# One quarter of w_in converted early, token groups changed every eight steps

## The chip, the core and the metric

One core of one Trainium2 chip runs the whole program in one launch. The metric is the device time of one execution in microseconds (us). The engines are TensorE (PE in the profile; PEld is its weight loads), VectorE (DVE), ScalarE (ACT), GpSimd (POOL) and SyncE (SP, which here only issues DMAs). Each engine runs its own instructions in the order in which they were written down, and they wait for each other by semaphores.

## The reference, cut to what matters

Three layers follow each other: windowed attention with 32 global tokens per batch, a soft mixture of experts, and a feed-forward layer whose weights w_in and w_out come as float64.

```python
# attention: 4 batches, 8 heads, 512 local + 32 global tokens, window 32
x = attention(q_l, k_l, v_l, q_g, k_g, v_g)      # (2176, 512)
logits = x @ phi                                 # 8 experts x 4 slots = 32 columns
slot_input = softmax(logits, 0).T @ x            # (8, 4, 512)
slot_out[e] = relu(slot_input[e] @ w1[e]) @ w2[e]
x = softmax(logits, 1) @ slot_out                # (2176, 512)
h = relu(x @ w_in)                               # w_in (512, 2048)
out = (h * h) @ w_out                            # w_out (2048, 512)
```

## The kernel before, in words

**Attention and the loads beside it.** The attention runs over 44 units of scores, exponent, transpose and product with V. The order of all work is the order of the code: tables tell after which unit a helper is emitted. In the shadow of the attention SP loads the expert weights in 64 pieces of 512 KB (`load_piece`, L581, in the order of the list `order`) into granules of 4 KB per partition. A granule is one place for one piece or one block; the lists in `room` hold the free ones: 16 of arena A, 8 and later more of arena B. Where no granule is free the load waits until a product has read one out.

**Conversion.** w_in and w_out arrive as float64 and are turned into single precision by five pieces of work (`convert`, L535): `split` (ACT, L540), `rest` (ACT L551 or DVE L553), `clamp` and `shift` (DVE, L543 and L546), and `join` (DVE L556, then an addition on POOL, L558). A w_out block is also cut into a high and a low half, `w_hl` (ACT L859, POOL L860). The left half of w_in, eight blocks of 128x512, is converted within the attention, at the units in `CONV` (L302), through one raw buffer: each block is loaded when the one before it is done.

**Experts.** `layer1` and `layer2` multiply the few slot rows with the 64 pieces; PE goes through 4 pieces at a time. After the last of them (`layer2(1, 6, 8)`) the result `so` is copied out, transposed (`layer2_T`) and becomes `slot_outT`. In `layer2` one idle product of 512 columns (L955) stands after the seventh of the eight parts.

**The last layer.** x is not built. G = slot_out @ w_in (32 rows) is split into a high and a low half and repeated (`G4`), so that one product gives a block of 128 features of h for 384 tokens. The work goes in 48 steps; a step is one token group (768, 768 or 640 tokens) with one of 16 blocks of features. `emit_h(n)` makes h of step n: a product (PE L1085), a relu (ACT L1088), a multiplication (DVE L1089); `emit_h_split(n)` cuts h*h into `ah` (ACT L1095) and `al` (DVE L1096). `emit_o(n)` then adds three products for each of six (or five) token tiles (PE L1140 to L1142) into six PSUM buffers. Round n of the loop holds `emit_h(n)`, then `emit_o(n-1)`, then what `plan[n]` holds of the conversions. `passes` (L1067) sets which group runs over which blocks; where a group stops before its last block its six sums are copied to `saved` and added later (L1147).

**What is converted there.** `seq` lists 24 raw blocks: eight of w_out, eight of w_in, eight of w_out. Block q begins in round q-2 (`split`, `rest`), goes on in round q-1 and, for w_out, ends in round q. `G_late` (L1027) makes the second half of G in two calls, at steps 11 and 15, and `replicate` (L1032) one eighth of G4 at a time. Both take a PSUM buffer of the pool `ps_h`, which has two and which the products of `emit_h` use as well.

Of the kernel before, what the change touches and what calls it, by code (L numbers as in the profile page):

```python
# [24 lines left out]
def local_global_attention__soft_moe__relu2_kernel(  # L25
# [51 lines left out]
    GR = 1024  # L77
# [31 lines left out]
    win_sb = A.carve(NC, FF // 2)  # L109
# [23 lines left out]
    room = {"a": A.granules(7, 23), "b": Bq.granules(10, 18), "t": []}  # L133
# [138 lines left out]
    for s in range(NJ):  # L272
# [29 lines left out]
    CONV = (4, 9, 13, 18, 22, 27, 31, 36)  # L302
    CONV_AT = (
        (0, 0, 1, 2, 3), (-1, 1, 1, 2, 3), (0, 0, 1, 2, 3), (0, 0, 0, 2, 3), (0, 1, 1, 2, 3), (0, 0, 0, 2, 3),
        (0, 1, 2, 2, 3), (0, 0, 1, 1, 2),
    )
    REST_ON_ACT = (0, 0, 1, 0, 1, 1, 1, 1)
# [5 lines left out]
        0, 0, 0, 0, 1, 2, 0, 0, 1, 1, 1, 1, 0, 1, 1, 1, 0, 0, 2, 2, 1, 0, 1, 1, 0, 1, 2, 1, 0, 1, 0, 0,  # L313
        3, 1, 0, 1, 1, 0, 1, 0, 4, 2, 2, 1,
# [262 lines left out]
    order.insert(62, ("raw", 0, 0))  # L577
# [3 lines left out]
    def load_piece():  # L581
# [8 lines left out]
        at = next((r for r in ("tba" if kind == 2 and e >= 4 else "tab") if room[r]), None)  # L590
# [25 lines left out]
    with tc.manual_schedule():  # L616
# [53 lines left out]
        for n in range(NC * WRES):  # L670
# [4 lines left out]
            if n + 1 < NC * WRES:  # L675
                after(u, win_load, n + 1, d=CONV_AT[n][-1])
# [5 lines left out]
        after(("l", 11, 1), give, "at", 6, 7, d=av_at(index["l", 11, 1]) - index["l", 11, 1] + MOE_D[2])  # L682
# [72 lines left out]
        free("at", 5, 6)  # L755
# [56 lines left out]
        tmp, = A.granules(4, 5)  # L812
# [12 lines left out]
        seq = [("o", m) for m in range(8)] + [("i", k) for k in range(2 * NC)] + [("o", m) for m in range(8, NFC)]  # L825
        plan = {}

        def raw_load():
            q = len(raws)
            if q == len(seq) or not room["a"]:  # L830
                return False
            raws[q] = g = room["a"].pop(0)
# [3 lines left out]
            else:  # L836
                f, c = WRES + k // NC, k % NC
# [7 lines left out]
        def put_convert(q, rest_on_act, first=False):  # L845
# [4 lines left out]
            else:  # L850
                f, c = divmod(k, NC)
# [10 lines left out]
            def last():  # L862
                join()
                room["a"].append(raws[q])
                raw_load()
# [346 lines left out]
```

## Time and profile before

| | us |
|---|---|
| median of 3 runs | 432.63 |
| lowest, highest | 430.64, 437.59 |
| the profiled execution's own time | 432.63 |
| its span | 430.2 |
| PE busy (share of the span) | 400.4 (93%) |
| DVE busy | 288.6 (67%) |
| ACT busy | 239.6 (56%) |
| POOL busy | 133.0 (31%) |

The span is the part of the profiled execution from its first to its last instruction. Busy PE contains products that overlap in the pipeline, so 93% is not a distance from a limit. The stages follow each other: attention to about 157 us, the passage to the experts to 169, the experts to 206, and from 210 on the last layer. The shares of busy time differ between them, so each is read by itself. A line number (L540) is one of the kernel before; the changed kernel's own numbers are a little different.

### The profile page before, as it was taken

What the parts mean: (1) busy time and instruction counts of PE and PEld (TensorE: products, weight loads), DVE (VectorE), ACT (ScalarE), POOL (GpSimd) and SP (SyncE); (2) the same over time, 40 slices, a digit from 0 to 9 for tenths busy, and PEclk for the clock granted to TensorE, in tenths of its full rate; (3) what the DMA queues carried; (4) which work ended last, traced back from release to release, by engine and by line L of the source; (5) the groups of instructions that cost most, each with busy time, mean ns of one, the idle gap of its engine ahead of it and who ended that gap; (6) DMA issues with size and microseconds to landing.
All of it is one profiled execution on the core that took longest, in us unless ns stands there. A gap on an engine that the chain in (4) does not pass through costs nothing.

```text
span 430.2 us, 12437 instructions
## 1 busy us (share of the span) xinstructions
PE 400.4 (93%) x4899; PEld 306.4 (71%) x4899; DVE 288.6 (67%) x930; ACT 239.6 (56%) x561; POOL 133.0 (31%) x159
## 2 busy tenths in 40 slices
PE   7789879989969978998999999999999999999996
PEld 6678667766757753354577877878877888888884
DVE  5597877768657866112599999778996545744443
ACT  3678768887867441221567666565754544444442
POOL 6245543644525531110345533234552000000000
PEclk9999999999989998999999999999999999999999
DMA  6888877899463698999913323300001500420003
GB/s 148 205 255 226 278 230 216 311 249 334 126 207 117 200 368 317 386 407 407 367 56 108 132 94 118 115 20 0 2 0 31 118 0 0 100 48 2 0 1 122
DMA packets 54890, 69.02 MB, mean 160 GB/s; under 512 B 23856, under 2 KB 40496, under 8 KB 54832
## 3 DMA queue, kind: packets, MB, share of 16 engines
q1 hardware_dynamic: 53360, 67.19, 48.2%
q10 hardware_dynamic: 1472, 1.05, 0.9%
q8 instruction: 38, 0.62, 0.6%
q14 instruction: 20, 0.16, 0.1%
HBM read 63.77 MB, written 4.46 MB: 159 GB/s over the span
## 4 chain that ended last, share of the span: by engine, by line
PE 62%; DVE 12%; DMA 11%; ACT 6%; issue 5%; SPq 1%; POOL 1%; POOLq 0%; ACTq 0%; DVEq 0%
PE ops L1140 9%; PE ops L1141 9%; PE ops L1142 9%; PE xp L391 5%; PE sp L330 5%; PE pp L372 4%; DMA arena_v<-in_v_l_dram 4%; DMA arena_a<-in_moe_w_out_dram 4%; PE hps L919 3%; PE tp L219 3%; PE ops L947 3%; DVE arena_a L543 3%; DMA arena_b<-in_moe_w_in_dram 3%; PE hp L1085 2%; ACT arena_b L146 2%
## 5 line engine op out<-in xcount | busy, mean ns | idle before, releaser
L1140 PE MATMUL ops<-w_hl,ah 128*128 128x512 f32 x271 | 107.2, 396 | 0.0
L1141 PE MATMUL ops<-w_hl,ah 128*128 128x512 f32 x271 | 106.3, 392 | 0.4 <-POOL w_hl L860 0.4
L1142 PE MATMUL ops<-w_hl,al 128*128 128x512 f32 x271 | 105.7, 390 | 0.0
L1089 DVE TENSOR_TENSOR arena_a<-hp,arena_a 128x384 f32<-128x384 f32 x96 | 46.8, 529 | 46.1 <-ACT arena_a L1088 46.0
L1088 ACT ACTIVATE arena_a<-hp 128x384 f32<-128x384 f32 x96 | 40.2, 471 | 66.0 <-PE hp L1085 65.9
L1095 ACT ACTIVATE ah<-arena_a 128x384 fp32r<-128x384 f32 x96 | 45.0, 505 | 25.9 <-DVE arena_a L1089 25.9
L1142 PEld LDWEIGHTS ops<-w_hl,al 128*128 128x128 f32 x271 | 50.9, 188 | 11.3 <-DVE al L1096 0.3
L1140 PEld LDWEIGHTS ops<-w_hl,ah 128*128 128x128 f32 x271 | 50.9, 188 | 11.0 <-issue 0.8
L1141 PEld LDWEIGHTS ops<-w_hl,ah 128*128 128x128 f32 x271 | 50.9, 188 | 10.5 <-POOL w_hl L860 1.8
L354 POOL TENSOR_TENSOR arena_r<-arena_b,nm 128x512 f32<-128x512 f32 x32 | 39.6, 1239 | 56.7 <-DVE nm L341 31.6
L1096 DVE TENSOR_TENSOR al<-arena_a,ah 128x384 fp32r<-128x384 f32 x96 | 49.9, 560 | 8.1 <-ACT ah L1095 4.2
L146 ACT ACTIVATE arena_b<-tp 64x256 f32<-64x256 f32 (+2 forms) x151 | 48.4, 347 | 9.3 <-PE tp L219 4.2
L558 POOL TENSOR_TENSOR arena_a<-arena_a 128x512 int32<-128x512 int32 x23 | 29.7, 1293 | 51.2 <-DVE arena_a L556 48.6
L341 DVE CUSTOM_DVE_ANT_0 arena_b<-sp,arena_r 128x128 f32<-128x128 f32 x128 | 29.5, 286 | 17.8 <-PE sp L330 11.9
L330 PE MATMUL sp<-arena_b 64*32 64x128 f32 x1024 | 36.0, 279 | 1.7 <-ACT arena_b L146 1.7
L391 PE MATMUL xp<-arena_v,arena_t 128*32 128x65 f32 x1408 | 27.6, 223 | 9.1 <-DMA arena_v<-in_v_l_dram 4.4
L364 ACT ACTIVATE arena_r<-arena_r 128x512 f32<-128x512 f32 x44 | 27.7, 630 | 10.5 <-POOL arena_r L354 10.2
L330 PEld LDWEIGHTS sp<-arena_b 64*32 64x32 f32 x1024 | 27.0, 110 | 9.1 <-issue 6.5
L372 PE MATMUL pp<-ident,arena_r 128*128 128x128 f32 x176 | 29.1, 289 | 4.4 <-ACT arena_r L364 4.4
L391 PEld LDWEIGHTS xp<-arena_v,arena_t 128*32 128x32 f32 x1408 | 22.4, 110 | 15.2 <-issue 11.0
L860 POOL TENSOR_TENSOR w_hl<-arena_a,w_hl 128x512 fp32r<-128x512 f32 x16 | 21.4, 1336 | 32.1 <-DMA arena_a<-in_moe_w_out_dram 16.2
L372 PEld LDWEIGHTS pp<-ident,arena_r 128*128 128x128 f32 x176 | 18.9, 142 | 10.9 <-ACT arena_r L364 5.4
(194 smaller groups left out, 589.5 us busy)
## 6 DMA issues: line engine op xcount, KB each, us to landing
arena_a<-in_moe_w_dram SPq DMA_DIRECT2D x35, 512.0 KB, 6.6
arena_b<-in_moe_w_dram SPq DMA_DIRECT2D x21, 512.0 KB, 7.2
arena_a<-in_moe_w_out_dram SPq DMA_DIRECT2D x16, 512.0 KB, 5.1
arena_v<-in_v_l_dram SPq DMA_DIRECT2D x16, 256.0 KB, 4.2
arena_b<-in_moe_w_in_dram SPq DMA_DIRECT2D x8, 512.0 KB, 4.9
arena_a<-in_moe_w_in_dram SPq DMA_DIRECT2D x8, 512.0 KB, 4.1
arena_k<-in_k_l_dram SPq DMA_DIRECT2D x30, 128.0 KB, 3.9
arena_q<-in_q_l_dram SPq DMA_DIRECT2D x30, 128.0 KB, 3.6
```

Source lines behind the costliest of these rows:

```text
L146: nc.scalar.activation(out=out, in_=in_, func=AF.Copy)
L330: nc.tensor.matmul(sp[r + 32 * e:r + 32 * e + 32, j], qz[d, (s + 2) % 3, hp, b], keys, start=True, stop=True, tile_position=(64 * e, r + 3 ...
L354: nc.gpsimd.tensor_tensor(out=pe.rearrange("p j (r k) -> p j k r", k=4), in0=s_buf.rearrange("p j (k r) -> p j k r", k=4), in1=nm.unsqueez ...
L372: nc.tensor.transpose(pp[:, j], pe_buf[n % NPE][:, j], ident)
L391: nc.tensor.matmul(xp[32 * b:32 * b + 32, 2 * h + e], p, V[:, b, 4 * half + 2 * h + e], start=True, stop=True)
L1088: nc.scalar.activation(out=r[:, :N], in_=hp[:, :N], func=AF.Relu)
L1089: nc.vector.tensor_tensor(out=a[:, :N], in0=hp[:, :N], in1=r[:, :N], op=ALU.mult)
L1095: nc.scalar.activation(out=ah[:, s], in_=a, func=AF.Copy)
L1096: nc.vector.tensor_tensor(out=al[:, s], in0=a, in1=ah[:, s].bitcast(F32), op=ALU.subtract)
L1140: nc.tensor.matmul(op, ah[:, s], w_hi, start=begin, stop=False)
L1141: nc.tensor.matmul(op, ah[:, s], w_lo, start=False, stop=False)
L1142: nc.tensor.matmul(op, al[:, s], w_hi, start=False, stop=end)
```

## The change

Only the first quarter of w_in (four blocks of 128x512) is converted within the attention. The other three quarters are converted in the last layer, which therefore has 28 blocks in `seq`: four of w_out, four of w_in, and so on in turn. Two granules of arena A that held w_in become room for pieces. The last layer changes token groups after 4, 8, 8, 8 and 4 steps, both of the first groups with partial sums. G is made in quarters, at steps 6, 14 and 22. The first block of w_out is loaded after all 64 pieces; `rest` of the last layer's blocks is always on ACT, and in round 3 two blocks begin at once.

```diff
-    win_sb = A.carve(NC, FF // 2)
+    CW = 512
+    win_sb = A.carve(NC, CW)
-    room = {"a": A.granules(7, 23), "b": Bq.granules(10, 18), "t": []}
+    room = {"e": [], "a": A.granules(10, 23), "b": Bq.granules(10, 18), "c": A.granules(5, 10), "t": []}
-    CONV = (4, 9, 13, 18, 22, 27, 31, 36)
+    CONV = (4, 9, 13, 18)
-    REST_ON_ACT = (0, 0, 1, 0, 1, 1, 1, 1)
+    REST_ON_ACT = (0, 0, 1, 0)
     PIECES = (
-        0, 0, 0, 0, 1, 2, 0, 0, 1, 1, 1, 1, 0, 1, 1, 1, 0, 0, 2, 2, 1, 0, 1, 1, 0, 1, 2, 1, 0, 1, 0, 0,
-        3, 1, 0, 1, 1, 0, 1, 0, 4, 2, 2, 1,
+        0, 0, 0, 0, 1, 2, 0, 0, 1, 1, 1, 1, 0, 1, 1, 1, 0, 0, 2, 2, 1, 1, 1, 1, 0, 2, 2, 1, 0, 1, 1, 0,
+        3, 1, 1, 0, 1, 0, 1, 1, 3, 1, 1, 1,
     )
-    order.insert(62, ("raw", 0, 0))
+    order.append(("raw", 0, 0))
...
-        seq = [("o", m) for m in range(8)] + [("i", k) for k in range(2 * NC)] + [("o", m) for m in range(8, NFC)]
+        seq = []
+        for f in range(NFC // 4):
+            if f:
+                seq += [("i", NC * f + c) for c in range(NC)]
+            seq += [("o", m) for m in range(4 * f, 4 * f + 4)]
...
-            a, b, c = q - 2, q - 1, q
+            b, c = a + 1, a + 2
...
-                if gr and c == 6:
-                    idle_products(1, ps_h, "h", c_flat[:, :512])
...
+        layer2(1, 2, 6)
...
+        put_convert(0, 0, True, True)
+        put_convert(1, 0, True)
+        now(("split", 0))
+        layer2(1, 6, 8)
+        while raw_load():
+            pass
+        now(("mask", 0), ("rest", 0))
...
         layer2_T(1)
+        now(("join", 0), ("split", 1), ("rest", 1))
...
+        sel = w_pool.tile([128, 2, 4, NS], F32R, name="sel")
+        nc.gpsimd.tensor_scalar(out=sel.rearrange("p a r s -> p (a r) s"), in0=blk.unsqueeze(1).to_broadcast([128, 8, NS]),
+                                scalar1=0.0, scalar2=None, op0=ALU.mult)
+        for r in range(4):
+            nc.gpsimd.tensor_copy(out=sel[:, r // 2, r], in_=blk)
+        now(("part", 0))
...
-        def G_late(j0, j1):
+        def G_late(f):
             gp = ps_h.tile([128, 256], F32, tag="h", name="gps")
-            G_part(1, gp, 0, NC, j0, j1)
-            G_split(1, gp, j0, j1)
+            G_part(f, gp, 0, NC)
+            G_split(f, gp)
...
-        passes = [(0, 0, 8), (1, 0, 16), (0, 8, 16), (2, 0, 16)]
+        passes = [(0, 0, 4), (1, 0, 8), (0, 4, 12), (1, 8, 16), (0, 12, 16), (2, 0, 16)]
-        late_at = {11: (0, 2), 15: (2, 4)}
+        late_at = {first_of[4 * f] - 2: f for f in range(1, 4)}
...
-                if t == 2 and n in late_at:
-                    G_late(*late_at[n])
-                if t == (4 if n == 0 else 3) and n in replicate_at:
+                if t == 1 and n in late_at:
+                    G_late(late_at[n])
+                if t == (4 if n == 0 or n in late_at else 3) and n in replicate_at:
                     replicate(replicate_at[n])
...
-                    if split and m == NFC - 1:
+                    if gi < 2 and (gi, 0, m + 1) not in passes:
                         nc.vector.tensor_tensor(out=o, in0=op, in1=o, op=ALU.add)
...
-            if n + 2 < len(seq):
-                put_convert(n + 2, n % 2 == 1 or n == 16)
+            for q in (n + 2,) if n < 3 else (5, 6) if n == 3 else (n + 3,):
+                if q < len(seq):
+                    put_convert(q, n, True)
...
-                for f in plan.pop(-5):
-                    f()
-                sel = w_pool.tile([128, 2, 4, NS], F32R, name="sel")
...
+                now(("mask", 1), ("join", 1))
+            if n == 1:
+                now(("part", 1))
```

SP's last loads before the stores, from the load into the freed V buffer on (arena_v), stand so before (moe_w holds w1 and w2):

```order
L599 DMA arena_v<-in_moe_w_dram 128x1024 x2
L599 DMA arena_b<-in_moe_w_dram 128x1024 x2
L599 DMA arena_t<-in_moe_w_dram 128x1024 x3
L599 DMA arena_a<-in_moe_w_dram 128x1024 x17
L599 DMA arena_b<-in_moe_w_dram 128x1024 x3
L533 DMA arena_a<-in_moe_w_out_dram 128x1024
L599 DMA arena_a<-in_moe_w_dram 128x1024
L599 DMA arena_t<-in_moe_w_dram 128x1024
L533 DMA arena_a<-in_moe_w_out_dram 128x1024 x7
```

and so in the changed kernel:

```order
L591 DMA arena_v<-in_moe_w_dram 128x1024 x2
L591 DMA arena_b<-in_moe_w_dram 128x1024 x2
L591 DMA arena_t<-in_moe_w_dram 128x1024 x3
L591 DMA arena_a<-in_moe_w_dram 128x1024 x17
L591 DMA arena_b<-in_moe_w_dram 128x1024 x2
L591 DMA arena_a<-in_moe_w_dram 128x1024
L531 DMA arena_a<-in_moe_w_out_dram 128x1024 x4
```

From V on, 30 loads end with the last piece before, and 27 now: two pieces fewer, and the w_out block behind them.

On ACT, rounds 2 to 4 of the last layer stood so before (L1088 is the relu, L1095 `ah`, L859 the high half of a w_out block, L540 `split`, L551 `rest`, G the copy of `replicate`):

```order
L1088 ACTIVATE arena_a<-hp 128x384 x2
L1095 ACTIVATE ah_3653<-arena_a 128x384 x2
L859 ACTIVATE w_hl<-arena_a 128x512
L540 ACTIVATE arena_a<-arena_a 128x512
L1088 ACTIVATE arena_a<-hp 128x384 x2
L1095 ACTIVATE ah_3651<-arena_a 128x384 x2
L146 ACTIVATE G_3648<-rps 128x256
L859 ACTIVATE w_hl<-arena_a 128x512
L540 ACTIVATE arena_a<-arena_a 128x512
L551 ACTIVATE arena_a<-arena_a 128x512
L1088 ACTIVATE arena_a<-hp 128x384 x2
```

and in the changed kernel rounds 3 to 5 so (L1095 is now the relu, L1102 `ah`, L856 the high half, L538 `split`, L549 `rest`, L147 the copies of the six sums):

```order
L1095 ACTIVATE arena_a<-hp 128x384 x2
L1102 ACTIVATE ah_3630<-arena_a 128x384 x2
L856 ACTIVATE w_hl<-arena_a 128x512
L538 ACTIVATE arena_a<-arena_a 128x512
L549 ACTIVATE arena_a<-arena_a 128x512
L538 ACTIVATE arena_a<-arena_a 128x512
L549 ACTIVATE arena_a<-arena_a 128x512
L1095 ACTIVATE arena_a<-hp 128x384 x2
L1102 ACTIVATE ah_3631<-arena_a 128x384 x2
L147 ACTIVATE arena_a<-ops 128x512 x3
L538 ACTIVATE arena_a<-arena_a 128x512
L549 ACTIVATE arena_a<-arena_a 128x512
```

Two pairs of `split` and `rest`, of blocks 5 and 6, stand ahead of the relu of round 4.

On DVE, the same place of the changed kernel (L1096 is the multiplication, L1103 `al`, L145 the copies of sums, L541 `clamp`, L544 `shift`, L554 `join`):

```order
L1096 TENSOR_TENSOR arena_a<-hp,arena_a 128x384 x2
L1103 TENSOR_TENSOR al_3634<-arena_a,ah_3631 128x384 x2
L145 COPY arena_a<-ops 128x512 x3
L541 TENSOR_SCALAR arena_a<-arena_a 128x512
L544 TENSOR_SCALAR arena_a<-arena_a 128x512
L554 SCALAR_TENSOR_TENSOR arena_a<-arena_a 128x512
L541 TENSOR_SCALAR arena_a<-arena_a 128x512
L544 TENSOR_SCALAR arena_a<-arena_a 128x512
L554 SCALAR_TENSOR_TENSOR arena_a<-arena_a 128x512
L1096 TENSOR_TENSOR arena_a<-hp,arena_a 128x384 x2
```

Between the multiplications of rounds 4 and 5 stand three copies and two conversions; before, no round had more than three copies and one conversion.

## Rows read from the trace of the kernel before

**Rows 1.** Busy time, 214 to 262 us: busy time (instructions), clock, DMA share, GB/s.
```profile
core 0: us, PE busy (x) PEld busy (x) DVE busy (x) ACT busy (x) POOL busy (x), PEclk, DMA share, GB/s
214.00:262.00 48.00, 47.79 (x213) 38.27 (x210) 45.25 (x80) 32.53 (x68) 22.34 (x21) 1.00 0.31 102
```

**Rows 2.** Timeline, ACT and PE in attention: start, us, operation, [idle before <-what ended it].
```profile
121.06 0.66 ACT L540 ACTIVATE arena_b<-arena_b 128x512 f32<-128x512 f32 x1 [3.85 <-DMA arena_b<-in_moe_w_in_dram]
...
122.29 1.12 PE L372 MATMUL pp<-ident,arena_r 128*128 128x128 f32 x4 [3.30 <-ACT arena_r L364]
```

**Rows 3.** Busy time of two stretches behind that wait, with the granted clock.
```profile
122.00:124.00 2.00, 1.71 (x8) 1.57 (x8) 0.60 (x2) 1.98 (x5) 0.00 (x0) 0.50 0.93 371
124.00:126.00 2.00, 2.00 (x54) 1.52 (x56) 0.04 (x1) 1.94 (x6) 0.00 (x0) 0.67 0.32 125
```

**Rows 4.** Chain that ended last, a stretch of layer2 without a wait.
```profile
186.10 3.59 PE ops L947 x64
```

**Rows 5.** Timeline of PE at the end of layer2.
```profile
200.50 0.80 PE L947 MATMUL ops<-arena_b,c_all 128*32 128x256 f32 x5
202.12 0.62 PE L947 MATMUL ops<-arena_a,c_all 128*32 128x256 f32 x2 [0.81 <-DMA arena_a<-in_moe_w_dram]
...
204.31 1.12 PE L268 MATMUL idle<-c_all,ident 128*128 128x512 f32 x2
...
206.06 0.38 PE L947 MATMUL ops<-arena_t,c_all 128*32 128x256 f32 x1
```

**Rows 6.** Busy time, 190 to 200 us, with the DMA rate.
```profile
190.00:200.00 10.00, 10.00 (x165) 6.30 (x167) 1.27 (x6) 1.48 (x4) 0.38 (x2) 1.00 1.03 407
```

**Rows 7.** Timeline of PE: first products (hp) of steps, and G_late (gps) in one.
```profile
247.26 0.51 PE L1085 MATMUL hp<-cstack,G 128*128 128x384 f32 x2
...
248.21 0.50 PE L1141 MATMUL ops<-w_hl,ah 128*128 128x512 f32 x1 [0.21 <-POOL w_hl L860]
...
252.18 0.51 PE L1085 MATMUL hp<-cstack,G 128*128 128x384 f32 x2
...
265.55 0.51 PE L1085 MATMUL hp<-cstack,G 128*128 128x384 f32 x2
...
267.92 1.92 PE L1019 MATMUL gps<-arena_a,slots 128*32 128x256 f32 x16 [0.48 <-DVE arena_a L1089]
...
272.63 0.51 PE L1085 MATMUL hp<-cstack,G 128*128 128x384 f32 x2
...
340.33 0.51 PE L1085 MATMUL hp<-cstack,G 128*128 128x384 f32 x2
...
344.77 0.51 PE L1085 MATMUL hp<-cstack,G 128*128 128x384 f32 x2
```

**Rows 8.** Timeline of DVE and POOL over steps with a conversion.
```profile
246.86 1.30 POOL L860 TENSOR_TENSOR w_hl<-arena_a,w_hl 128x512 fp32r<-128x512 f32 x1 [0.74 <-ACT w_hl L859]
...
246.92 1.52 DVE L543 TENSOR_SCALAR arena_a<-arena_a 128x512 f32<-128x512 f32 x1
...
249.75 1.01 DVE L1089 TENSOR_TENSOR arena_a<-hp,arena_a 128x384 f32<-128x384 f32 x2
...
253.82 0.41 DVE L543 TENSOR_SCALAR arena_a<-arena_a 128x512 f32<-128x512 f32 x1
...
255.33 1.02 DVE L1089 TENSOR_TENSOR arena_a<-hp,arena_a 128x384 f32<-128x384 f32 x2
...
259.39 1.01 DVE L1089 TENSOR_TENSOR arena_a<-hp,arena_a 128x384 f32<-128x384 f32 x2
...
263.18 1.02 DVE L1089 TENSOR_TENSOR arena_a<-hp,arena_a 128x384 f32<-128x384 f32 x2
...
266.29 0.42 DVE L553 TENSOR_SCALAR arena_a<-arena_a 128x512 int32<-128x512 uint32 x1
...
267.23 1.01 DVE L1089 TENSOR_TENSOR arena_a<-hp,arena_a 128x384 f32<-128x384 f32 x2
```

**Rows 9.** Costliest groups, 210 to 430 us: busy us, mean ns of one | idle.
```profile
L1147 DVE TENSOR_TENSOR arena_a<-ops,arena_a 128x512 f32<-128x512 f32 x6 | 3.7, 682 | 0.0
```

More of the change, by code (lines that the diff above doesn't have):

```diff
@@ L589, in load_piece @@
             return raw_load()
-        at = next((r for r in ("tba" if kind == 2 and e >= 4 else "tab") if room[r]), None)
+        at = next((r for r in ("tcba" if kind == 2 and e >= 4 else "tcab") if room[r]), None)
         if at is None:
@@ L669, in local_global_attention__soft_moe__relu2_kernel @@
                     at(l1, pos, fn, i, d=d + dd)
-        for n in range(NC * WRES):
+        for n in range(NC):
             split, clamp, shift, rest, join = win_convert(n)
@@ L829, in raw_load @@
             q = len(raws)
-            if q == len(seq) or not room["a"]:
-                return False
-            raws[q] = g = room["a"].pop(0)
+            at = next((r for r in "ae" if room[r]), None)
+            if q == len(seq) or at is None:
+                return False
+            g = room[at].pop(0)
+            raws[q] = g, at
             kind, k = seq[q]
@@ L850, in put_convert @@
             else:
-                f, c = divmod(k, NC)
-                o = win2[c][:, CW * f:CW * f + CW]
-            split, clamp, shift, rest, join = convert(raws[q].rearrange("p (n w) -> p n w", w=2).bitcast(I32),
+                o = w_block(*divmod(k, NC))
+            split, clamp, shift, rest, join = convert(raws[q][0].rearrange("p (n w) -> p n w", w=2).bitcast(I32),
                                                       o.bitcast(I32), y[:, 0:DM], y[:, DM:].bitcast(I32),
@@ L863, in last @@
                 join()
-                room["a"].append(raws[q])
+                g, at = raws[q]
+                if at == "a":
+                    room["a"].append(g)
                 raw_load()
-            a, b, c = q - 2, q - 1, q
-            if first:
-                a, b, c = -1, -1, -2
-            if q == 1:
-                put(-2, [split, rest])
-                put(-3, [clamp, shift])
-                put(-4, [last])
-                put(-5, [part])
+            b, c = a + 1, a + 2
+            if q < 2:
+                for name, fs in zip(("split", "rest", "mask", "join", "part"),
+                                    ([split], [rest], [clamp, shift], [last], [part])):
+                    put((name, q), fs)
                 return
```

89 lines of the change are left out of this document (37 added, 52 removed).

## The prediction, made before the changed kernel had run

> **What bounds the kernel now.** I read the busy times by stage first. In the last layer PE is busy in 47.79 of 48.00 us at a granted clock of 1.00, and DVE in 45.25 [rows 1]: PE sets the time there, and DVE has almost nothing to spare as long as blocks are converted. A step without anything beside its products takes 344.77 − 340.33 = 4.44 us [rows 7]; I call this 4.45. The reader should see that all gain in the last layer must come from waits, of which there are few, and that a DVE which falls behind becomes the bound at once.
>
> In attention the timeline shows one large wait: ACT waits 3.85 us for a w_in block from DMA, and PE in turn 3.30 [rows 2]. Behind it the granted clock is 0.50 and 0.67, with the DMA at 371 GB/s in the first of the two stretches [rows 3]. At the experts' end, DMA is the limit: 407 GB/s with all engines' share full [rows 6], and PE waits for pieces [rows 5]. 512 KB at 407 GB/s are 1.29 us.
>
> **The change part by part.**
>
> *Attention.* Four w_in blocks are no longer loaded and converted; pieces take their places in the DMA queue. The wait of rows 2 goes: 3.30 us. The low clock behind it goes too: busy 1.71 at 0.50 and 2.00 at 0.67 lose (1 − 0.50) × 1.71 + (1 − 0.67) × 2.00 = 1.5 [rows 3]. Of these 4.8 I take 4.0, since PE would then meet the next load earlier. Bounds: −2.0 (a following load takes most of it) and −5.5 (the small waits at the other three blocks too). **−4.0.**
>
> *End of layer2.* From 201.0 to 206.44 are 5.4 us [rows 5], in which 32 records are left; 64 take 3.59 where nothing is waited for [rows 4], so 32 take 1.8. The other 3.6 are waits for pieces and the idle product (1.12, removed). In SP's list 27 loads end with the last piece from V on, where there were 30: 3 × 1.29 = 3.9 us shorter, enough for 3.6. The list starts when attention gives V free, so the 4.0 above move it and PE alike, and the 3.9 come on top. Bounds: −1.1 (only the idle product) and −3.8. **−3.6.**
>
> *From there to the first products of the last layer.* Nothing is taken away from PE: the halved product of G uses half of PE's columns at once and its instructions run less side by side. The first w_out block now lands last, at least 1.29 after the last piece, and PE needs about 1.8 after that piece; so it should be just in time. `sel` is made earlier on POOL and can hold up a clamp. Bounds −0.5 and +1.5, the second a clamp of 1.52 instead of 0.41 [rows 8] and a little more. **0.**
>
> *Waits for `w_hl`.* From block 5 on the conversion begins three rounds ahead instead of two. Before, a product waits for POOL's low half [rows 7], and the step takes 252.18 − 247.26 = 4.92 instead of 4.45. There are four such steps; this one costs 0.47, the four together 1.4. Bounds 0 and −1.4. **−1.4.**
>
> *G in quarters.* Three calls instead of two. The step with a call takes 272.63 − 265.55 = 7.08, or 2.63 over a clean one, of which 0.48 is a wait for the buffer behind the multiplication [rows 7]; without that wait 2.1. The call now stands one tile (0.71, a sixth of a step) earlier. With the multiplication as late as there (267.23 − 265.55 = 1.68 [rows 7, 8]) it waits 0.48 + 0.71 = 1.2, so 3.3 each at steps 6 and 22; I give the one at step 14 2.3, where DVE has caught up. 8.9, against 2.6 + 2.1 = 4.7 before. Bounds: +1.5 (DVE early, 3 × 2.1) and +6. **+4.2.**
>
> *Two conversions in round 3.* On DVE the multiplications of rounds 4 and 5 are now separated by three copies and two conversions. The nearest rows: a round with one conversion, no `rest`, takes 263.18 − 259.39 = 3.79; with three copies 255.33 − 249.75 = 5.58; the second conversion adds 255.33 − 253.82 = 1.51; a clamp beside POOL's `w_hl` takes 1.52 instead of 0.41, 1.1 more [rows 8]. Rounds 3 to 5: (3.79 + 1.1) + (5.58 + 1.51 + 1.1) = 13.1, against two steps of 8.9: DVE falls back by 4.2. It starts at 1.68 less the `rest` of 0.42 that is on ACT now [rows 8], 1.3, and ends at 5.5. A lag of 255.33 − 252.18 = 3.15 is seen to cost nothing [rows 7, 8]; a whole step, 4.45, cannot be free, since the next products need the same buffers. I take 3.5: **PE waits 2.0.** Besides, ACT runs in order: `rest` of block 6 needs the buffer that POOL's addition of block 4 reads, and the relu of round 4 stands behind it. Addition 1.30 (as the POOL row over the same shape), a pass of ACT 0.66 [rows 2, 8] and half a relu, about 0.45 by that pass: 2.4 in which DVE stands still, and PE with it. Bounds: +1.8 (a lag up to 4.45 is free) and +6. **+4.4.**
>
> *Sums added after step 19.* Six additions of 0.68 [rows 9], 4.1, in a round with a conversion: 1.2 + 3.79 + 4.1 − 4.45 = 4.6 of lag, 1.1 above 3.5. Those after steps 31 and 35 meet a DVE without conversions and are hidden by the step; if not, they are still late by less than a step and are caught up before the next. Bounds 0 and +2. **+1.0.**
>
> All `rest`s on ACT: by one pass of 0.66 in a step where ACT has a third of its time free (32.53 of 48.00 busy [rows 1]). **0**, as long as no relu has to wait for it (rival below).
>
> Sum: −4.0 − 3.6 + 0 − 1.4 + 4.2 + 4.4 + 1.0 = +0.6. The profiled execution took 432.6, the same as the median of the runs: **433**. All bounds together reach from about 425 to 444.
>
> **The rivals.**
>
> *The lag is absorbed.* If a lag of almost a step is free and G's calls find their buffer, the losses are 1.5 + 1.8 + 0 and the gains 9.0: −5.7, or 427. For it: DVE's rounds without `rest` take 3.79, so it recovers 0.65 in each step. Against it: three copies and two conversions in one round have no precedent here.
>
> *The gain in attention only moves.* DMA is at 371 GB/s in attention's bad stretch and at 407 behind it; if the pieces do not in fact come earlier because no granule is free when SP could load, PE arrives early and waits longer at the end: 433 + 4 = 437. That is also the case in which the change does not do what it says.
>
> *The clock.* PE stands still for about 3 us around steps 5 and 6. Behind the 3.30 us of rows 2 the clock is at 0.50 [rows 3], the lower of its two levels, 1.2 GHz; the shorter waits at the end of layer2 (0.81 [rows 5]) have no such trail. If these stalls are of the first kind, 1.5 to 2.5 are added by rows 3: 435 to 436. The Trainium skill, "TensorE: Matmul & The Clock Gate", section "HAM oscillation — how this bites in real kernels", says that an idle gap puts the array back to its lower level and the products behind it pay; by that rule this rival would be the forecast. Rows 3 agree with the rule, but the stall here comes in pieces with products between them.
>
> *Slower: ACT becomes the bound.* Every conversion's `split` and `rest` now stand ahead of the next round's relu on ACT, and `rest` has to wait for POOL's addition of the block two before it. With one block begun per round that addition belongs to the round before; if DVE lags so far that the addition is late in every round, relu starts late in every round, the multiplication behind it later still, and nothing is caught up. The price is what DVE no longer recovers plus what ACT adds: 4.45 − 3.79 − 1.1 = −0.44 in a round with a blocked clamp [rows 7, 8], so 0.4 in each of some 25 rounds: +10, 443. It decides from the point at which relu starts over 2.5 us after its product, the free lag of 3.5 less the multiplication's own 1.0. For it: ACT gets 14 or so more `rest`s of 0.66 each within some 110 us. Against: only one round begins two blocks, ACT has a third of its time free [rows 1], and the clamp is blocked only where a w_out block is converted.
>
> **How the numbers follow.** The forecast (losses and gains as above, 430 to 436) gets 0.42, the absorbed lag (424 to 430, about half of it below 424.5) 0.24, the moved gain 0.12, the clock 0.13, ACT as bound 0.09. 2% are 8.65 us (424.0 and 441.3), about what a measurement of this kernel can tell from no change. Faster by more: half of the absorbed lag and a trace of the forecast, 0.13. Slower by more: most of the last rival, the upper ends of the two before it, 0.12. Within: 0.75. The range 425 to 441 leaves out about a tenth at each end.
>
> **What would show it.** Right: no ACT wait for w_in near 118 to 122 us and a clock near 1.00 there; the end of layer2 about 7.6 us earlier without DMA waits; at steps 4 to 6 first products that wait for a multiplication, and the relu of round 4 behind `rest`; three `gps` groups, the first and last with a wait for the buffer; no product waiting for `w_hl` from POOL; a wait around step 20. Wrong: if steps 4 to 6 are 4.45 long (then the losses were too dear), if layer2 still waits for pieces, or if most steps are longer than 4.45 with ACT as releaser.

## The result, and the profile after

The changed kernel takes 437.45 us (median of 21 runs, 433.17 to 445.65), the kernel before 433.44 in the same comparison (21 runs, 429.73 to 438.38). The ratio is 1.012, with a 95% interval of 1.0088 to 1.0152: slower, by less than the 2% of the prediction's classes. The prediction was 433, with a range of 425 to 441, and no change as the likeliest.

The trace of the kernel before is 427.14 us long, that of the changed kernel 428.63, up to the end of the last copy of sums; cut at the same places:

| stretch | before | after | difference |
|---|---|---|---|
| to the last product with V | 157.48 | 153.77 | −3.7 |
| from there to the first product of layer1 | 11.64 | 10.03 | −1.6 |
| from there to the first product of G | 38.75 | 34.93 | −3.8 |
| from there to step 0 | 2.48 | 2.08 | −0.4 |
| steps 0 to 3 | 18.20 | 18.37 | +0.2 |
| steps 4 to 7 | 18.72 | 27.71 | +9.0 |
| steps 8 to 15 | 39.33 | 39.52 | +0.2 |
| steps 16 to 23 | 39.90 | 41.42 | +1.5 |
| steps 24 to 31 | 36.07 | 36.22 | +0.1 |
| step 32 to the end | 64.58 | 64.58 | 0.0 |

A ratio is taken over undisturbed executions alone (of the kernel before, 6 of 29 where e1, e2, e3 and e5 below are compared), and the traces of e2 and e10, by its time also that of b1, are of disturbed, longer ones, so that of e2 and e10 only the last layer is read.

So in these two traces 9.5 us are gained ahead of the last layer and 11.0 lost in it. The trace of the changed kernel is one of its shortest executions (433.58 us, the lowest is 433.17), that of the kernel before (432.63) lies near its median; the two differ by less than the medians do, and the part on attention below says where. The end of layer2, in PE's timeline of the changed kernel, answers to [rows 5]: the first product of layer1, the last groups of products of layer2 and the first of G.

```profile
163.80 1.50 PE L915 MATMUL hps<-arena_a,slots 128*32 128x512 f32 x12 [0.38 <-DVE slots L795]
...
196.91 0.39 PE L943 MATMUL ops<-arena_b,c_all 128*32 128x256 f32 x2
...
198.73 1.95 PE L1057 MATMUL gd<-arena_a,slots 128*32 128x128 f32 x64
```

No product of layer2 waits for a piece any more. The loss is in the timeline of PE over steps 4 to 7, beside the steps of [rows 7] (hp is the first product of a step, gps the late G, rps the handing-out of G; the calls that the prediction has at steps 6, 14 and 22 belong to the sums of these steps, which run during steps 7, 15 and 23):

```profile
219.18 0.51 PE L1092 MATMUL hp<-cstack,G 128*128 128x384 f32 x2
...
220.09 0.50 PE L1148 MATMUL ops<-w_hl,ah 128*128 128x512 f32 x1 [0.17 <-POOL w_hl L857]
...
224.60 0.91 PE L1092 MATMUL hp<-cstack,G 128*128 128x384 f32 x2 [0.34 <-DVE arena_a L1096]
226.10 0.50 PE L1147 MATMUL ops<-w_hl,ah 128*128 128x512 f32 x1 [0.60 <-ACT arena_a L147]
...
232.68 0.90 PE L1092 MATMUL hp<-cstack,G 128*128 128x384 f32 x2 [2.21 <-DVE arena_a L1096]
...
239.19 0.51 PE L1092 MATMUL hp<-cstack,G 128*128 128x384 f32 x2
...
240.85 1.92 PE L1031 MATMUL gps<-arena_a,slots 128*32 128x256 f32 x16 [0.45 <-DVE arena_a L1096]
...
244.97 0.49 PE L1049 MATMUL rps<-ghl,sel 32*128 32x256 f32 x2
```

Steps 4, 5 and 6 take 5.42, 8.09 and 6.51 us where a clean one takes 4.45. In step 5 the wait is plain: 2.21 for DVE's multiplication. Step 6 has no wait behind its first product and is 2.06 too long; the busy times of the stretches behind the wait say why (columns as in [rows 3]):

```profile
232.00:234.00 2.00, 1.29 (x5) 0.81 (x5) 1.80 (x4) 1.75 (x5) 1.27 (x1) 0.96 0.63 164
234.00:236.00 2.00, 2.00 (x6) 1.61 (x6) 1.93 (x5) 1.56 (x4) 0.07 (x1) 0.50 0.50 195
236.00:238.00 2.00, 2.00 (x7) 1.58 (x7) 1.87 (x4) 1.71 (x4) 1.22 (x1) 0.68 0.00 0
```

PE is busy all the time, at a granted clock of 0.50 and 0.68. What DVE does meanwhile stands in its timeline of rounds 4 and 5:

```profile
223.99 1.02 DVE L1096 TENSOR_TENSOR arena_a<-hp,arena_a 128x384 f32<-128x384 f32 x2 [2.47 <-ACT arena_a L1095]
...
226.08 1.88 DVE L145 COPY arena_a<-ops 128x512 f32<-128x512 f32 x3
...
229.40 0.42 DVE L541 TENSOR_SCALAR arena_a<-arena_a 128x512 f32<-128x512 f32 x1
229.85 1.39 DVE L544 TENSOR_SCALAR arena_a<-arena_a 128x512 int32<-128x512 int32 x1
...
232.07 1.02 DVE L1096 TENSOR_TENSOR arena_a<-hp,arena_a 128x384 f32<-128x384 f32 x2
```

and what ACT does ahead of the relu that DVE waits for (L538 and L549 are `split` and `rest` of block 6, L1095 the relu of round 4):

```profile
221.55 0.67 ACT L538 ACTIVATE arena_a<-arena_a 128x512 f32<-128x512 f32 x1 [1.78 <-DVE arena_a L554]
222.91 0.66 ACT L549 ACTIVATE arena_a<-arena_a 128x512 int32<-128x512 uint32 x1 [0.70 <-POOL arena_a L556]
223.48 0.85 ACT L1095 ACTIVATE arena_a<-hp 128x384 f32<-128x384 f32 x2
```

The reader is to see the chain: `split` waits for DVE's `join` of block 4, `rest` for POOL's addition of it, the relu stands behind both, and DVE waits 2.47 us for the relu. Then DVE does three copies and two conversions, and 8.08 us lie between its multiplications of rounds 4 and 5.

### The profile page after: what moved, and what is told of

Its sections match the earlier page's. It is cut to its first block, busy times and chain, and to the rows that moved or that the text cites. A ratio compares the mean times of both kernels' runs of the same rounds, so it can differ in the third digit from the quotient of the medians.

```text
span 431.6 us, 12415 instructions
## 1 busy us (share of the span) xinstructions
PE 400.6 (93%) x4897; PEld 305.5 (71%) x4897; DVE 292.6 (68%) x934; ACT 245.3 (57%) x571; POOL 132.9 (31%) x159
## 4 chain that ended last, share of the span: by engine, by line
PE 68%; DVE 14%; ACT 7%; DMA 5%; issue 3%; POOL 1%; ACTq 1%; DVEq 0%; POOLq 0%
PE ops L1147 11%; PE ops L1149 10%; PE ops L1148 10%; PE sp L328 5%; PE xp L389 5%; DMA arena_v<-in_v_l_dram 4%; PE pp L370 4%; PE ops L943 3%; PE hps L915 3%; DVE al L1103 3%; PE hp L1092 3%; ACT arena_b L147 3%; PE tp L220 2%; PE sp L334 2%; DVE arena_a L541 2%
## 5 line engine op out<-in xcount | busy, mean ns | idle before, releaser
L1096 DVE TENSOR_TENSOR arena_a<-hp,arena_a 128x384 f32<-128x384 f32 x96 | 46.8, 529 | 43.5 <-ACT arena_a L1095 43.3
L1095 ACT ACTIVATE arena_a<-hp 128x384 f32<-128x384 f32 x96 | 40.1, 471 | 51.7 <-PE hp L1092 51.7
L1102 ACT ACTIVATE ah<-arena_a 128x384 fp32r<-128x384 f32 x96 | 44.9, 504 | 24.6 <-DVE arena_a L1096 24.6
L1103 DVE TENSOR_TENSOR al<-arena_a,ah 128x384 fp32r<-128x384 f32 x96 | 51.6, 577 | 8.9 <-ACT ah L1102 4.9
L147 ACT ACTIVATE arena_b<-tp 64x256 f32<-64x256 f32 (+2 forms) x151 | 48.6, 349 | 9.9 <-PE tp L220 4.9
L556 POOL TENSOR_TENSOR arena_a<-arena_a 128x512 int32<-128x512 int32 x27 | 34.9, 1293 | 60.1 <-DVE arena_a L554 53.8
L1092 PE MATMUL hp<-cstack,G 128*128 128x384 f32 x96 | 25.2, 337 | 3.6 <-DVE arena_a L1096 2.5
```

The source lines that it names most:

```text
L147: nc.scalar.activation(out=out, in_=in_, func=AF.Copy)
L1095: nc.scalar.activation(out=r[:, :N], in_=hp[:, :N], func=AF.Relu)
L1096: nc.vector.tensor_tensor(out=a[:, :N], in0=hp[:, :N], in1=r[:, :N], op=ALU.mult)
L1102: nc.scalar.activation(out=ah[:, s], in_=a, func=AF.Copy)
L1103: nc.vector.tensor_tensor(out=al[:, s], in0=a, in1=ah[:, s].bitcast(F32), op=ALU.subtract)
```

## The experiments

Steps in us, from the first product of one step to that of the next (e1, e2 and so on are the experiments below). Across the traces the same step of the same code agrees within 0.1 where nothing was changed nearby, so here one trace of each is enough; attention varies between executions of the same instructions.

| step | before | after | e1 | e2 | e3 | e5 | e8 | e10 |
|---|---|---|---|---|---|---|---|---|
| 1 | 6.75 | 7.77 | 7.77 | 7.77 | 7.77 | 7.77 | 6.34 | 7.77 |
| 2 | 4.45 | 4.58 | 4.58 | 4.57 | 4.58 | 4.58 | 5.69 | 4.58 |
| 4 | 4.45 | 5.42 | 4.94 | 4.89 | 4.93 | 5.43 | 4.89 | 4.92 |
| 5 | 5.09 | 8.09 | 4.45 | 6.22 | 6.13 | 8.08 | 4.45 | 4.45 |
| 6 | 4.45 | 6.51 | 4.45 | 6.54 | 6.30 | 4.91 | 4.45 | 4.65 |
| 7 | 4.73 | 7.69 | 8.46 | 7.71 | 11.47 | 8.79 | 7.05 | 8.17 |
| 15 | 5.07 | 7.69 | 8.43 | 7.73 | 7.70 | 7.71 | 6.43 | 7.30 |
| 21 | 5.13 | 4.59 | 5.39 | 4.56 | 4.59 | 4.45 | 4.71 | 5.21 |
| 22 | 4.47 | 5.16 | 5.16 | 5.18 | 5.17 | 5.00 | 5.20 | 5.15 |
| 23 | 4.65 | 8.78 | 8.73 | 8.75 | 8.78 | 8.78 | 7.33 | 7.58 |
| 0 to 31 | 152.2 | 163.2 | 159.7 | 160.9 | 164.4 | 162.5 | 156.9 | 157.3 |

(Late G stands in steps 12 and 16 before, 7.07 and 6.52 long, and in 7, 15 and 23 after.)

**e1: one block per round.**

```diff
-            for q in (n + 2,) if n < 3 else (5, 6) if n == 3 else (n + 3,):
+            for q in (n + 2,):
```

> The changed kernel with one block begun per round all the way (block n+2 in round n); round 3 no longer begins two, and no block has the extra round of slack. In the changed kernel steps 4 to 6 take 5.42 + 8.09 + 6.51 = 20.02 us where three clean ones take 13.35. Theory (the second conversion in rounds 3 and 4 is what holds DVE and, through ACT's order, the relu): steps 4 to 6 come down to 14 to 15 us, the clock stays at 1.00 there, but a product waits for POOL's low half of w_out again (about 1.4 us in all) and the call of G at step 6 may wait for the last addition (up to 1.5): 3 to 4.5 us shorter in all than the changed kernel. Rival (DVE is simply full in this region; the three copies and the blocked clamps cost it anyway): steps 4 to 6 stay above 17 us, and the total within 2 us of the changed kernel.

Steps 4 to 6 take 13.84 us instead of 20.02, and no stretch of them waits but 0.19 for POOL's low half. The calls of G wait 1.20, 1.21 and 1.47 instead of 0.45, 0.47 and 1.52. Over all steps it is 3.6 us shorter, as the theory said, not 6.2: with the head start of one round gone too, steps 7, 15 and 21 are 2.3 longer. The ratio to the kernel before is 1.0059 (1.0004 to 1.0114), and the plain medians, 436.50 and 436.58, do not differ. The two conversions at once, not DVE's load as such, made the stall in steps 4 to 6.

**e2: the relu ahead of the second `split` and `rest`.** In round 4 `split` of block 6 is written behind `emit_h(4)` and its `rest` behind `emit_h_split(4)`.

```diff
...
+                if n == 4:
+                    now("s6")
                 if n != 1:
                     emit_h_split(n)
+                if n == 4:
+                    now("r6")
```

> The changed kernel with the split and rest of block 6 put behind the relu and behind ah of round 4 on ACT; the same work, two blocks still begin at once. Theory with ACT's order as a part of the stall: the 2.47 us in which DVE waits for the relu before the multiplication of round 4 go, PE's wait of 2.21 us before step 6 shrinks to under 1, and the clock no longer falls behind it: steps 4 to 6 from 20.0 to about 16 us. Rival (the lag of DVE alone, two conversions and three copies in a row): DVE's wait goes but PE's wait before step 6 stays near 2 us, and steps 4 to 6 stay above 19.

The multiplication of round 4 no longer waits, and PE's wait before step 6 is 1.61 instead of 2.21, in the timelines of DVE and PE:

```profile
234.31 1.02 DVE L1100 TENSOR_TENSOR arena_a<-hp,arena_a 128x384 f32<-128x384 f32 x2
```

```profile
243.18 0.91 PE L1096 MATMUL hp<-cstack,G 128*128 128x384 f32 x2 [1.61 <-DVE arena_a L1100]
```

Steps 4 to 6 take 17.65, 2.4 less, the size that the prediction gave to ACT's order. The rest of the theory missed: the wait did not fall under 1, and the clock fell behind it all the same in this trace (0.50 in 245 to 247 us). Both parts of the prediction's term are there, and taking one away leaves the other. The ratio is 1.0055 (1.0015 to 1.0095), the plain medians are 437.31 and 436.58.

**e3: two blocks begin in round 4, not in round 3.**

```diff
-            for q in (n + 2,) if n < 3 else (5, 6) if n == 3 else (n + 3,):
+            for q in (n + 2,) if n < 4 else (6, 7) if n == 4 else (n + 3,):
```

> The changed kernel with two blocks (6 and 7) begun in round 4 instead of blocks 5 and 6 in round 3; the second conversion then lies on DVE in round 5, where no sums are copied. Theory with two parts (copies and conversions together 2.0 us, ACT's order 2.4): the part of the copies goes, ACT's order still holds the relu of round 5 behind the second rest: steps 4 to 7 about 2 us shorter than in the changed kernel (27.7 there). If ACT's order is all: no change. If the meeting of copies and second conversion is all: 4 us shorter or more.

Steps 4 to 7 take 28.83, 1.1 longer, so all three cases missed. The timeline of DVE shows the wait of 2.5 for a relu moved by one round, and that of PE shows three waits, the last at the call of G:

```profile
236.50 1.02 DVE L1096 TENSOR_TENSOR arena_a<-hp,arena_a 128x384 f32<-128x384 f32 x2 [2.53 <-ACT arena_a L1095]
```

```profile
237.12 0.91 PE L1092 MATMUL hp<-cstack,G 128*128 128x384 f32 x2 [1.53 <-DVE arena_a L1096]
...
243.41 0.91 PE L1092 MATMUL hp<-cstack,G 128*128 128x384 f32 x2 [1.24 <-DVE arena_a L1096]
...
247.21 3.31 PE L1031 MATMUL gps<-arena_a,slots 128*32 128x256 f32 x16 [2.12 <-DVE arena_a L1096]
```

A lag that ends one round later has one round less to be caught up before G's call takes its buffer: the wait there is 2.12 instead of 0.45, and the products of G run at a granted clock of 0.50 (3.31 instead of 1.92). That this is the reason is argued from the one trace. What the copies cost in that round can't be told from this. The ratio is 1.0108 (1.004 to 1.0176).

**e5: half of the additions after step 19 on ACT and POOL.**

```diff
+                        if n == 19 and t % 2:
+                            nc.scalar.activation(out=o_buf[t // 2], in_=op, func=AF.Copy)
+                            nc.gpsimd.tensor_tensor(out=o, in0=o_buf[t // 2], in1=o, op=ALU.add)
+                        else:
...
```

> The changed kernel with three of the six additions after step 19 made by ACT (copy to a free buffer) and POOL (addition) instead of DVE; DVE saves three times 0.61 us. In the changed kernel steps 20 to 22 and the call of G behind them are 4.59, 5.16 and 8.78 us, 1.9 over clean steps and the other two calls (7.69). Theory (DVE's lag after the additions makes these): 1.4 to 1.9 us shorter. Rival (POOL's additions hold up DVE's instructions as they do a clamp, 1.1 each): within 0.5 us.

Steps 20 to 23 are 0.3 shorter: the rival. DVE's timeline of the changed kernel, six additions, `clamp` and `shift`:

```profile
308.17 3.67 DVE L1154 TENSOR_TENSOR arena_a<-ops,arena_a 128x512 f32<-128x512 f32 x6
311.76 0.42 DVE L541 TENSOR_SCALAR arena_a<-arena_a 128x512 f32<-128x512 f32 x1
312.21 0.43 DVE L544 TENSOR_SCALAR arena_a<-arena_a 128x512 int32<-128x512 int32 x1
```

and the timelines of DVE and POOL of this kernel:

```profile
309.92 1.87 DVE L1158 TENSOR_TENSOR arena_a<-ops,arena_a 128x512 f32<-128x512 f32 x3
311.71 0.98 DVE L541 TENSOR_SCALAR arena_a<-arena_a 128x512 f32<-128x512 f32 x1
312.73 1.40 DVE L544 TENSOR_SCALAR arena_a<-arena_a 128x512 int32<-128x512 int32 x1
```

```profile
309.73 4.12 POOL L1156 TENSOR_TENSOR arena_a<-arena_a 128x512 f32<-128x512 f32 x3 [0.61 <-ACT arena_a L1155]
```

DVE's additions fall from 3.67 to 1.87, and `clamp` and `shift` beside POOL's additions grow from 0.42 and 0.43 to 0.98 and 1.40: of 1.80 saved 1.53 are given back. The Trainium skill, "SBUF — State Buffer", section "SBUF: two separate sides", says that VectorE and GpSimd share a port pair which one of them holds for a whole instruction, where VectorE's operation is in a 2-port mode, or has two inputs in SBUF and GpSimd's reads SBUF. The rows agree as far as they go: DVE's additions, with one input in PSUM (`ops`), stay at 0.62 each beside POOL's, and `clamp` and `shift` are lengthened; in which mode these two run no row shows. The ratio of this kernel is 1.019 (1.012 to 1.0261), above that of the changed kernel, but the plain medians, 439.81 and 436.58, give 1.0074; whether it is slower than the changed kernel is not shown.

The same trace holds an answer on the clock that was not asked for. PE waits 2.20 before step 6, as in the changed kernel, but the clock stays at 1.00 (all stretches from 232 to 242 us):

```profile
234.95 0.91 PE L1092 MATMUL hp<-cstack,G 128*128 128x384 f32 x2 [2.20 <-DVE arena_a L1096]
...
242.58 1.92 PE L1031 MATMUL gps<-arena_a,slots 128*32 128x256 f32 x16 [1.51 <-DVE arena_a L1096]
```

Step 6 takes 4.91 instead of 6.51, and the call of G in step 7 waits 1.51 instead of 0.45. Steps 4 to 7 take 27.21 against 27.71: by these two traces DVE catches up while the clock is low, and what the clock takes is mostly time that PE would wait a step later.

**e6: the kernel before without the last four loads of w_in** (the work on these blocks stays).

```diff
-                after(u, win_load, n + 1, d=CONV_AT[n][-1])
+                if n + 1 < 4:
+                    after(u, win_load, n + 1, d=CONV_AT[n][-1])
```

> The kernel before, but the last four of the eight w_in blocks of the attention are not loaded; their conversion still runs, on the block loaded before (that quarter of w_in is not what the reference has). It takes the load and its wait away and leaves the work. In the five traces of the changed kernel and its variants so far the last product with V starts at 153.8, 158.8, 166.8, 160.8 and 156.3 us though the attention is the same instructions, 157.5 in the one trace of the kernel before. Theory of the prediction (that wait cost 4.0 us in each execution): the median is 3 to 5 us below the kernel before. Rival (the wait of that one trace is one of several that come and go, and the gain in attention was luck of one execution): the median within 1.5 us of the kernel before.

The median is 435.29 against 435.96, the ratio 0.9972 (0.9923 to 1.0022): 1.2 us by the ratio, and the interval holds none as well as 3.3. The long wait is gone, and PE's idle time from 10 us to the end of attention is what it was, 17.3 us up to 155 against 17.2 up to 157. The last product with V is at 155.2 all the same, against 157.5, by less busy time (127.70 against 129.81): the granted clock of 120 to 130 us is 1.00 and not 0.83. This trace is of the shortest execution, 429.69 us. The waits by line, of the kernel before and of this one (us in total, times, longest):

```profile
PE xp L391 <- DMA arena_v<-in_v_l_dram: 4.4, 4, 2.1
PE pp L372 <- ACT arena_r L364: 4.4, 4, 3.3
PE xp L391 <- issue: 2.6, 4, 1.3
```

```profile
PE xp L391 <- DMA arena_v<-in_v_l_dram: 3.8, 4, 1.9
PE sp L330 <- issue: 3.5, 2, 2.7
...
PE pp L372 <- ACT arena_r L364: 1.2, 2, 1.0
```

"issue" is a wait for nothing that the profile shows; in this trace waits of that kind and small ones stand where the removed one stood in the sum.

**e7: the tail of the experts alone, in the kernel before.**

```diff
-    order.insert(62, ("raw", 0, 0))
+    order.append(("raw", 0, 0))
...
-                if gr and c == 6:
-                    idle_products(1, ps_h, "h", c_flat[:, :512])
```

> The kernel before with two things of the change alone: the first w_out block is loaded after all pieces and the idle product in layer2 is gone. From the first product of layer1 to the first of G the kernel before takes 38.75 us, the changed kernel and all its variants 34.92 to 34.93. Theory (waits for the last pieces and the idle product, 3 loads of 1.29 fewer ahead of them): with one load fewer 1.3 us and the 1.1 of the idle product go as far as they don't overlap: 36.4 to 37.5. Rival (only the idle product counts, the pieces then bound it again): 38.0 or more; rival (two pieces come early enough by the single load): under 35.5. The total 1 to 2.5 us below the kernel before.

Missed: the stretch takes 39.52 us, longer than before, and the ratio is 1.0006 (0.996 to 1.0051). The products do end earlier, 34.7 us after the first of layer1 instead of 37.3 (33.5 in the changed kernel). What follows takes it back, in ACT's, DVE's and PE's rows of one timeline after another:

```profile
205.20 0.67 ACT L540 ACTIVATE arena_a<-arena_a 128x512 f32<-128x512 f32 x1 [6.03 <-DMA arena_a<-in_moe_w_out_dram]
```

```profile
205.90 0.43 DVE L543 TENSOR_SCALAR arena_a<-arena_a 128x512 f32<-128x512 f32 x1 [6.29 <-ACT arena_a L540]
...
208.27 0.42 DVE L144 COPY arena_a<-ops 128x256 f32<-128x256 f32 x1
```

```profile
208.74 1.11 PE L961 MATMUL otp<-ident,arena_a 128*128 128x128 f32 x4 [2.25 <-DVE arena_a L144]
```

The first w_out block now lands last, its conversion is written ahead of the copy of `so` on DVE, and the copy stands behind it. The changed kernel writes the conversion's DVE part behind that copy, so the later load costs it nothing. The later load and the later conversion belong together here; the new instruction order alone was not tried.

**The kernel before, once more.**

> The kernel before, unchanged, once more with a trace. If its attention also ends at another time than 157.5 us (by 2 us or more, with waits that nothing in the profile explains), the 4 us that the first two traces differ in attention are no effect of the change. If it ends within 1 us of 157.5, they are. From layer1 on the theory expects the same times within 0.3 us.

The last product with V is at 159.0 us, 1.5 later than in the first trace, between the two cases. The wait for the load is there again (the timelines of ACT and PE):

```profile
122.46 0.66 ACT L540 ACTIVATE arena_b<-arena_b 128x512 f32<-128x512 f32 x1 [3.59 <-DMA arena_b<-in_moe_w_in_dram]
```

```profile
123.69 1.12 PE L372 MATMUL pp<-ident,arena_r 128*128 128x128 f32 x4 [3.08 <-ACT arena_r L364]
```

From layer1 to G it takes 40.30 us, not 38.75, and the busy times of 169 to 180 us show the lower clock and a DMA that waits (0.58, 191 GB/s):

```profile
169.00:180.00 11.00, 10.20 (x66) 3.57 (x69) 3.81 (x12) 0.53 (x2) 0.64 (x2) 0.58 0.54 191
```

The expectation of 0.3 missed there. The last layer agrees within 0.04.

**e8: G by four column groups.** On top of e1, each quarter of G in four groups of 128 columns, at the third tile, handed out one block at a time.

```diff
...
-                for j in range(2):
-                    r = 64 * (f % 2) + 32 * j
-                    nc.tensor.matmul(gp[r:r + 32], slot_outT[:, c], w_block(f, c)[:, 256 * j:256 * j + 256],
+                for j in range(4):
+                    nc.tensor.matmul(gp[32 * j:32 * j + 32], slot_outT[:, c], w_block(f, c)[:, 128 * j:128 * j + 128],
...
-        replicate_at = {first_of[2 * i] - 2: i for i in range(1, 8)}
+        replicate_at = {first_of[m] - 2: m for m in range(2, 16)}
...
-                if t == 1 and n in late_at:
+                if t == 2 and n in late_at:
...
```

> The changed kernel with one block begun per round (as in the first experiment) and each quarter of G made in four column groups of 128 instead of two of 256, one tile later (third instead of second), handed out one block of 128 at a time. Theory: a call takes 0.98 us of PE instead of 1.92 (64 records of 128 columns in four groups take 1.95), its wait for the buffer shrinks by the tile, 0.71; three calls: 2.8 + 2.1 us less than in the first experiment, so 154 to 156 us from the first step to step 32 (159.7 there, 163.2 in the changed kernel, 152.2 before). With the 5.9 us gained ahead of the last layer it would be 2 to 4 us below the kernel before. Rival (the smaller portions cost as much in waits for the two buffers as they save): 158 us or more, total not below the kernel before.

Steps 0 to 31 take 156.9, between theory and rival. In PE's timeline a call takes 1.29, not 0.98, and its wait is 0.50 (1.20 in e1); a handing-out of one block costs its step 0.58, twice as often as two blocks cost 0.65:

```profile
241.41 1.29 PE L1030 MATMUL gps<-arena_a,slots 128*32 128x128 f32 x32 [0.50 <-DVE arena_a L1093]
...
244.21 0.43 PE L1046 MATMUL rps<-ghl,sel 32*128 32x128 f32 x2
```

The median is 434.91 against 435.96, the ratio 1.0002 (0.9958 to 1.0046): as the kernel before.

**e10: two blocks handed out at a time again.** The handing-out multiplies 64 rows by a selection `selp` that holds one of two rows of blocks; POOL makes it in rounds 4 and 5.

```diff
...
+                for j in range(2):
+                    for a in range(2):
+                        nc.tensor.matmul(rp[:, 128 * j:128 * j + 128], selp[r, j, a].rearrange("p r s -> p (r s)"),
+                                         gl4[r, a], start=(a == 0), stop=(a == 1))
...
```

> As the kernel with four column groups (one block begun per round, a quarter of G in four groups of 128 columns at the third tile), but G is handed out two blocks at a time again, 7 times instead of 14, by products over 64 rows with two masked selections made on POOL in rounds 4 and 5. In the kernel with four column groups each handing-out of one block lengthens its step by 0.58, so 13 of them cost 7.5 where 7 of two blocks cost 0.65 each, 4.6. Theory: from the first step to step 32 about 153.5 to 154.5 us (156.9 there, 152.2 before), step 2 back at 4.6 (5.69 there), and the total 2 to 4 us below the kernel before, since 5.6 us are gained ahead of the last layer. Rival (the masked selections on POOL hold up DVE in rounds 4 to 6, and the products over 64 rows take twice the time): 156 us or more, the total as the kernel before.

Steps 0 to 31 take 157.3: the rival's time in the last layer. G's first call waits 1.35, behind DVE work that lasts longer beside POOL's 2.48 us of `selp` (`al` 1.47, `clamp` 0.62), the handing-out costs 0.82 instead of 0.65, and step 1 is back at 7.77, since the first quarter of G is made in two groups again. POOL's and PE's timelines:

```profile
240.20 2.48 POOL L1202 CAST selp<-sel 32x256 fp32r<-32x256 f32 x4
```

```profile
247.78 1.29 PE L1045 MATMUL gps<-arena_a,slots 128*32 128x128 f32 x32 [1.35 <-DVE arena_a L1108]
```

Yet the ratio is the lowest of all: 433.17 us (13 runs) against 434.85, 0.996 (0.9921 to 0.9998). It is below 1 by little more than the interval, 1.6% below the changed kernel's ratio, and its interval overlaps that of e8, so that nothing shows which of the two is the faster.

## Why the prediction was right

The range held and the sign was open, as said. The median lies 4 us above the predicted time, and also above the 430 to 436 that the forecast's own case was given: two of the rivals, the gain that only moves and the clock, came in part together, and that the range held is owed to its width as much as to the terms. (Its bounds added up reach 445, not 444.) Each term can be set beside what the runs gave.

*Attention, −4.0: mis-sized.* The wait itself is real. It is 3.30, 3.08 and 3.03 us in the three traces of programs that have that load, and missing in all others. The low clock of [rows 3] is gone at that place too:

```profile
122.00:124.00 2.00, 2.00 (x43) 1.63 (x40) 1.25 (x6) 1.12 (x2) 1.16 (x2) 1.00 1.00 395
124.00:126.00 2.00, 1.48 (x27) 1.05 (x25) 1.12 (x10) 1.18 (x3) 0.83 (x1) 1.00 0.81 218
```

but the same trace has 0.83 in 10 to 20 us and 0.85 in 80 to 90, where the first has 1.00. What failed is the step from the wait to the time: PE arrives earlier at loads and at "issue" waits that follow. The last product with V is at 157.5, 159.0 and 159.9 us in the first and in b1 and e7 (mean 158.8), and at 153.8, 158.8, 160.8, 156.3 and 159.7 in the changed kernel, e1, e3, e5 and e8 (mean 157.9). So the change is worth about 0.9 by these few traces (1.4 with e6's 155.2 counted among those without the load) and 1.2 by e6's ratio; the spread of the traces alone would not rule out 4.0, e6's interval, 3.3 at most, does. A part of the spread can be seen. ACT waits 3.21 to 4.00 us for an earlier w_in block, near 57 us, in the first trace, e6, e7 and b1, and 3.01, 3.35 and 4.00 in e1, e3 and e8; the changed kernel and e5, whose attention ends first of the five, have no such wait. That load belongs to both kernels, so the 3.7 between the first two traces is in part the luck of one execution. What became of the wait is the rival in which the gain only moves, with another place for it than I gave: within attention, not at the pieces. Waits of this kind, of the changed kernel by line:

```profile
PE xp L389 <- DMA arena_v<-in_v_l_dram: 4.2, 3, 2.4
PE sp L328 <- issue: 1.9, 2, 1.6
...
PE sp L328 <- DVE cm L500: 1.3, 1, 1.3
```

*From there to layer1, not in the sum: about −1.0.* The first two traces differ by 1.6. Where the granted clock is 1.00 throughout, the stretch takes 11.20 in e6 and 11.22 in e7, and 9.8 to 10.5 in the changed kernel, e1, e3, e5 and e8. In e6 and e7 PE has an "issue" wait of 1.3 or 1.4 there, in those five of 0.5 at most; why is open. The first trace has a clock of 0.85 there (11.64 us), b1 0.71 (13.60).

*End of layer2, −3.6: right, −3.8.* 34.92 or 34.93 us in six traces of changed kernels, against 38.75 before. That needed the order of the first conversion as well as the loads, as e7 shows, where the products end 2.6 earlier and nothing is left of it; the prediction had seen the conversion only as a risk of +1.5.

*To the first step, 0: −0.4,* and then +0.7 in steps 0 and 1 (9.35 against 8.62), inside the bounds.

*Waits for `w_hl`, −1.4: about −0.9.* The four old ones are gone (1.4 by the steps), but one new pair remains: steps 2 and 4 are 0.13 and about 0.45 too long even in e1 and e2, with POOL as the releaser of the wait that shows in step 4 (0.17, in e1 0.19).

*G in quarters, +4.2: right in its sum.* The three steps with a call take 24.16, the same steps without one would take 3 × 5.10 with a handing-out: 8.9, as predicted, against 4.7. The split was different, and that the sums agree so well is luck. The waits are 0.45, 0.47 and 1.52 where I had 1.2, 0.2 and 1.2, since DVE has caught up at step 6 and has not at step 22:

```profile
321.77 1.92 PE L1031 MATMUL gps<-arena_a,slots 128*32 128x256 f32 x16 [1.52 <-DVE arena_a L1096]
```

*Two conversions in round 3, +4.4: right in its mechanism, 6.2 in size* (20.02 − 3 × 4.45 − 0.45 for the wait for `w_hl` in step 4). ACT's order is worth the 2.4 foreseen (e2), and both parts are gone with one block per round (e1). The part that was missing is the clock, a rival of its own in the prediction: 0.50 and 0.68 after the wait of 2.21. It is not simply added, as e5 shows: without it the two kernels differ by 0.5 over steps 4 to 7. The same wait of 2.2 us was followed by the lower clock in one trace and by the higher in the other. The rule of the Trainium skill that the prediction weighed ("TensorE: Matmul & The Clock Gate", section "HAM oscillation — how this bites in real kernels"), that an idle gap puts the array back to its lower level, agrees with the first trace and not with the second; the measurement decides, and it says sometimes.

*Additions after step 19, +1.0: +0.9* in steps 20 to 22 (14.20 against 13.35), and about 1.1 of the wait at G's call at step 22.

The rival with ACT as the bound did not come: outside the round with two conversions no step is longer than 4.45 for it. With attention at −1.0 instead of −4.0 and the two conversions at 6.2 instead of 4.4, the predicted sum of +0.6 becomes +5.4. By stages, as measured, −1.0 (attention), −1.0 (to layer1), −3.8, −0.4 and +11.0 (the last layer) make +4.8; the ratio of 1.012 gives +5.2, the medians +4.0.

## What to carry to other kernels

A wait that stands in every trace is worth its length only if nothing behind it is ready to take its place: take the wait away alone, and time that, before counting on it. Where one trace of each kernel is at hand, terms from a stretch that repeats to 0.1 us may be summed; a stretch in which the same program varies by several us carries no term of that size from one trace. When one engine gets two pieces of a chain per round, look at what stands behind the second piece in each in-order queue and where its buffer comes from, not only at the busy time.

## What the runs showed of the hardware

POOL's work on tiles of SBUF lengthens DVE's: `shift` took 1.39 or 1.40 us beside a POOL addition and 0.43 alone, so that moving three additions from DVE to POOL freed 1.80 us of DVE, took back 1.53, and made the steps 0.3 shorter. The same attention code ended between 157.5 and 159.9 us in three traces, with waits of PE that nothing in the profile releases of 2.6 to 4.4 us in all. A wait of PE of 2.2 us was followed by the lower clock in one trace and by the full clock in another. Products of 32 rows in four column groups of 128 took 1.29 us for the 32 records of one quarter of G where two groups of 256 took 1.92, not half.
